# A chunked delta-rule kernel with a max-of-three feed-forward layer: a reordered opening, and 38 extra products of the identity on TensorE

## The chip, the core and the metric

The kernel runs on one core of a Trainium2 chip. A core has a matrix engine (TensorE, "PE"; its weight loads are listed as "PEld"), three engines that work element by element (VectorE "DVE", ScalarE "ACT", GpSimd "POOL"), SyncE ("SP") that only issues transfers, and DMA queues that any of them but VectorE and TensorE fill here. Each engine takes its instructions in the order of the program; between engines, semaphores keep order. The metric is the time in device microseconds (us) of one execution.

## What is computed

Inputs are q, k, v of shape (4, 8, 768, 48), that is batch, heads, steps, and width of a head, beta of shape (4, 8, 768), and four weight matrices.

```python
k_n = k / (np.linalg.norm(k, axis=-1, keepdims=True) + 1e-06)
for t in range(S):
    kt, vt, bt = (k_n[:, :, t], v[:, :, t], beta[:, :, t, None])
    y[:, :, t] = np.einsum('bhd,bhde->bhe', q[:, :, t], state)
    v_old = np.einsum('bhde,bhd->bhe', state, kt)
    state = state + bt[:, :, :, None] * np.einsum('bhd,bhe->bhde', kt, vt - v_old)
...
x = y.transpose(0, 2, 1, 3).reshape(B * S, H * D)          # 3072 tokens of 384
h = np.maximum(np.maximum(x @ w1, x @ w2), x @ w3)         # width 768
out = h @ w_out
```

Everything is in 32-bit floating point, except that the weights arrive as 64-bit numbers and are converted on the chip.

## The kernel before

**Chunks.** The 768 steps are cut into 12 chunks of 64 (`C`), two of which form one of 6 groups. Within a chunk the recurrence becomes matrix products and the inverse of a unit triangular matrix, made of the products of the chunk's keys. All 32 pairs of batch and head go through together. Group m is prepared while the feed-forward layer of an earlier group runs on TensorE; for group 0 nothing runs beside it, and its preparation is the opening of the kernel, from the first load to the first feed-forward product `p_h` (L1224) at 44.9 us.

**The order** is written out by hand (`manual_schedule`, L104 on). The lines L1281 to L1375 are the opening; then the loop over `ffn(0)` yields after each product of hidden units, and the tables `LINKS` and `FIRST` say which steps of the recurrence and of the next preparation are put in at each yield. The program's order is each engine's order.

**Preparing a unit.** `load_k`, `load_q` bring keys and queries of unit n (a chunk and half of the batches); `turn` (L322) transposes them on TensorE (against the identity `ident`) and copies the result out as `kqt`; part 0 is the keys, part 1 the queries. `gram` (L404) multiplies keys with keys into `at` (part 0) or keys with queries into `pt` (part 1). With `later=True` ACT copies `pt` out and the `mask` is applied later by `masked` (L398); otherwise VectorE masks straight from PSUM.

**The triangular solve.** `solve(m)` (L507) works on blocks of 32x32. For the group 0, `to_blocks` and `first_blocks` put the products into `x_bl`, 128 partitions x 32 x 32. Its diagonal holds the squared norms of the keys. `norm` (L268) makes the norm: a root on ACT, then on VectorE a Newton step and the added 1e-6 of the reference. Its inverse square times beta scales `x_bl` (L547) and starts the diagonal of `y_bl`. Group 0 then takes 15 steps (`HB` = 16, so two halves of 16) of two VectorE instructions each (L561, L565). After them y_bl is transposed (L573) and `placed` (L498) copies it into `ut[0]` and `ut[1]`, the two chunks' triangular matrices. The halves are joined to 32 by `halves_t` (VectorE transposes), `halves_z` and `halves_u` (TensorE products `p_e`, `p_f`, with copies), then to 64 by `turn_t1`, `join_z` and `join_u` (`p_z`, `p_j`). Later groups take 31 steps and go through DRAM: `blocks(m)` loads their blocks, for group 1 into a spare part of the weights' tile (`in_wo`).

**A chunk's step.** `scale` multiplies v by the norms on POOL (`nrm_0` for the first two chunks, made by `first_norms`); `new` makes u (`p_u`), `to_y` the outputs (`p_y`), `to_x` transposes them (`p_x`) into `xt`, the feed-forward input; `step` adds to the state `st` (`p_s`, L801), `old_k` subtracts the state's share from v (`p_k`, L755), `old_q` keeps that of the queries (`p_q`).

**Weights.** Each of 24 pieces is fetched as raw bits (`fetch`), taken apart by three ACT instructions (L247 to L249), and put together by a VectorE shift (L259) and a POOL add (L263), `joined`. The generator `weights()` is `conv`: `some(conv, 1)` does the ACT part of a piece and then joins the piece before it. `p_h` of a yield needs its piece joined.

**Fillers that exist already.** `busy(n, of)` (L1290) runs n products of the identity into a PSUM tile `p_w` that nobody reads; it is called once, with 6, before the first transposition. `p_w` shares its two PSUM buffers with `p_h`.

Of the kernel before, what the change touches and what calls it, by code (L numbers as in the profile page):

```python
# [18 lines left out]
BL = 32  # L19
# [4 lines left out]
def kernel(  # L24
# [205 lines left out]
    def weights():  # L230

        waiting = None
        for dst, _, (a, b) in pieces:
            bits = staged.popleft().rearrange("p (a b two) -> p a b two", a=a, two=2)
            low, high = bits[:, :, :, 0], bits[:, :, :, 1]
            mant = work.tile([128, 384], U32, name="mant", bufs=2)
            up = work.tile([128, 384], I32, name="up", bufs=2)
            mant_v = mant.rearrange("p (a b) -> p a b", a=a)  # L240
            up_v = up.rearrange("p (a b) -> p a b", a=a)
            halves = [
                up.bitcast(t)[:, i::2].rearrange("p (a b) -> p a b", a=a)
                for i, t in enumerate((I16, FP16))
            ]

            nc.scalar.mul(mant_v.bitcast(FP32), high.bitcast(FP32), 2.0**-112)  # L247
            nc.scalar.mul(halves[0], low, 2.0**-29)
            nc.scalar.mul(halves[1], high.bitcast(FP32), 2.0**-64)  # L249
            if waiting:  # L250
                joined(*waiting)
            waiting = dst, mant, mant_v, up_v
            yield
        joined(*waiting)
        yield
# [12 lines left out]
    def norm(out, ksum, root, t):  # L268
# [8 lines left out]
        )  # L277

# [219 lines left out]
    def placed(cc, i, copy=nc.vector.tensor_copy, xs_of=slice(0, 2 * H)):  # L498
# [6 lines left out]
        copy(to[:, xs_of], of[:, xs_of])  # L505

    def solve(m):  # L507
# [14 lines left out]
        norm(bl, diagonal(x), small("root_bl", BL), small("nt_bl", BL))  # L522
        if m == 1:
            y = ps_two("y_p").rearrange("p b (j i) -> p (b j) i", i=BL)
            nc.scalar.copy(y, zero.to_broadcast(y.shape))
        if m:
            norms_of(m, bl)
            nc.vector.reciprocal(bl, bl)
        else:
            bl_0.append(bl)  # L530
            bl = small("inv_bl", BL)
            nc.vector.reciprocal(bl, bl_0[0])
        nc.vector.tensor_tensor(out=bl, in0=bl, in1=bl, op=ALU.mult)
        nc.vector.tensor_tensor(out=bl, in0=bl, in1=beta_bl[:, m] if m else beta_0, op=ALU.mult)
# [36 lines left out]
        if m == 0:  # L571
            back = in_rows(xs[0])
            nc.vector.transpose(out=back, in_=y.rearrange("p c i -> p i c"))  # L573
            yield
            for i in range(4):
                if i % 2:
                    n = H * (i == 3)
                    if n:
                        placed(0, i, nc.vector.tensor_copy, slice(0, n))
                    placed(0, i, nc.scalar.copy, slice(n, 2 * H))  # L580
                else:
                    placed(0, i, nc.vector.tensor_copy)
            return
# [55 lines left out]
    def halves_t(c, parts=(0, 1)):  # L639
        if c not in fine:  # L640
            fine[c] = [square("t") for g in range(2)]
        src = [ut[c % NU][:, g].rearrange("p h x -> p (h x)") for g in range(2)]
        dst = [t.rearrange("p h x -> p (h x)") for t in fine[c]]
        if 0 in parts:
            nc.vector.transpose(out=dst[0], in_=src[0])
        for bb in range(2) if 1 in parts else ():
            nc.vector.transpose(out=dst[1][rows(1 - bb)], in_=src[1][rows(bb)])
# [27 lines left out]

    def halves_z(c):
        if c > 1:
            halves_t(c)
        at = [ats[2 * c + g] for g in range(2)]
        second = ut[c % NU].rearrange("p g h (f two x) -> p g h f two x", two=2, x=HB)  # L680
        for hs, p_v, copy in heads_of(c, "p_e", BL):
# [6 lines left out]
            copy(zs[c % NU][:, :, span(hs)], p_v)  # L688
# [601 lines left out]
    def busy(n, of):  # L1290
        p_w = ps_ffn([128, TOK], "p_w")[:, 0 : of.shape[1]]
        for _ in range(n):
            nc.tensor.matmul(p_w, ident, of)

# [35 lines left out]
    turn(6, (0,))  # L1330
    turn(0, (1,))
    load_q(3, (nc.gpsimd, nc.gpsimd))
    load_beta()
    keys(6)
    gram(0, (1,), None, later=True)
    turn(7, (0,))
    turn(1, (1,))
# [3 lines left out]
    turn(3, (1,))  # L1341
    some(conv, 1)
    gram(2, (1,), None, later=True)
    gram(3, (1,), None, later=True)
    some(solving, HB + 1)
    halves_t(0)
    halves_z(0)
    first_norms()
    some(conv, 1)
    placed(1, 0)  # L1350
    scale(0, nrm_0[:, 0])
    placed(1, 1, nc.gpsimd.tensor_copy)
    blocks(1, nc.gpsimd)
    for _ in range(2):
        fetch(nc.gpsimd)
    halves_u(0)
    turn_t1(0)
    join_z(0)
    masked(pts[0], by_par(pts[0]))
    placed(1, 2)  # L1360
    join_u(0)
    masked(pts[1], by_par(pts[1]))
    old_k(0)
    old_q(0)
    new(0)
    some(conv, 1)
    fetch(nc.gpsimd)
    load_v(1, nc.gpsimd)
    placed(1, 3)
    to_y(0)  # L1370
    halves_t(1)
    solving = solve(1)
    some(solving, 1)
    to_x(0)
    some(conv, 1)  # L1375
# [76 lines left out]
    for i, _ in enumerate(ffn(0)):  # L1452
# [11 lines left out]
        if i == 25:  # L1464
            some(conv, 1)
# [7 lines left out]
        if i in CONVERTED:  # L1473
            some(conv, 1)
        if i == 0:
            fetch(nc.gpsimd)
# [78 lines left out]
```

## Time and profile before

| | |
|---|---|
| median of three runs | 506.24 us (505.86 to 509.44) |
| the profiled execution | 506.9 us, span 505.2 us |
| mean granted TensorE clock | 0.968 |
| busy: PE, PEld, DVE, ACT, POOL | 484.0, 338.0, 361.1, 169.4, 187.1 us |
| first `p_h` product | 44.92 us |
| granted clock 0.50 | 18.96 to 22.38 and 25.79 to 53.1 us |

All times of the trace count from the first instruction of the span. A view by windows gives the busy time of each engine in a stretch and the clock that TensorE was granted. A timeline gives start, length, engine, line, operation, output<-input by the program's names, shape and, in brackets, the idle time of the engine before it and what ended it. A view of waits names the waiting and the releasing instruction, total time, how often, and the longest.

### The profile page before, as it was taken

The page shows a single profiled execution, that of the slowest core. Times are in us where ns is not written, and L with a number is a line of the kernel's source. Part 1 is how long each engine was busy: PE and PEld are TensorE (multiplying, and loading weights), DVE is VectorE, ACT ScalarE, POOL GpSimd, SP SyncE. Part 2 cuts the span into 40 slices and gives each one's busy share as a digit, 9 for nine tenths or more (in the row PEclk, how much of TensorE's full clock was granted, in tenths as well). Part 3 has the DMA queues.
Part 4 walks back from the last instruction along what each step waited for, and adds up shares of the span by engine and source line. Part 5 has one row for each costly group of instructions (what it writes and reads, how often), then busy time and mean ns, then how long its engine had stood idle before and what let it go on. Part 6 is the DMA issues. An engine that isn't in the chain of part 4 may idle for free.

```text
span 505.2 us, 18676 instructions
## 1 busy us (share of the span) xinstructions
PE 484.0 (96%) x8064; PEld 338.0 (67%) x8064; DVE 361.1 (71%) x835; ACT 169.4 (34%) x320; POOL 187.1 (37%) x311
## 2 busy tenths in 40 slices
PE   7678989999999999999999999999999999999996
PEld 6467767855566555565565565555797457998895
DVE  5888799787996441799652999565998874468753
ACT  5585664885422142210152200242201032212210
POOL 7434472793391935770395880501000020000000
PEclk9855899999999999999999999999999999999999
DMA  8937869864045934544584652744224230340002
GB/s 114 205 50 214 195 142 160 198 181 137 3 120 134 191 72 77 146 119 117 112 156 104 158 137 74 149 72 96 64 54 90 47 86 15 85 94 1 0 18 47
DMA packets 109121, 53.50 MB, mean 106 GB/s; under 512 B 92208, under 2 KB 102864, under 8 KB 109040
## 3 DMA queue, kind: packets, MB, share of 16 engines
q1 hardware_dynamic: 97280, 31.78, 31.0%
q0 software_dynamic: 9216, 19.85, 16.5%
q8 instruction: 63, 1.03, 0.9%
q10 hardware_dynamic: 2544, 0.69, 0.8%
q14 instruction: 18, 0.15, 0.1%
HBM read 39.17 MB, written 13.11 MB: 103 GB/s over the span
## 4 chain that ended last, share of the span: by engine, by line
PE 76%; DVE 11%; ACT 4%; DMA 3%; SPq 3%; issue 2%; POOL 0%; DVEq 0%; ACTq 0%; POOLq 0%
PE p_h L1224 28%; PE p_o L985 13%; PE p_o L1262 12%; PE p_c L1163 5%; DVE tmp L561 3%; PE p_g L415 2%; PE p_m L905 2%; PE p_u L771 2%; PE p_k L743 2%; DVE y_p L565 2%; DMA kmore<-in_k_dram 2%; PE p_y L813 2%; PE p_s L794 2%; PE p_q L743 1%; PE p_j L726 1%
## 5 line engine op out<-in xcount | busy, mean ns | idle before, releaser
L1224 PE MATMUL p_h<-xt,w_sb 128*128 128x512 f32 (+1 forms) x450 | 186.8, 558 | 0.6 <-ACT xt L839 0.6
L1224 PEld LDWEIGHTS p_h<-xt,w_sb 128*128 128x128 f32 x450 | 82.4, 193 | 69.2 <-issue 61.6
L1238 DVE TENSOR_TENSOR h<-h,p_h 128x512 f32<-128x512 f32 (+1 forms) x42 | 25.5, 607 | 46.8 <-PE p_h L1224 46.3
L565 DVE TENSOR_TENSOR y_bl<-y_bl,tmp 128x31 f32<-128x31 f32 (+20 forms) x139 | 50.4, 363 | 4.8
L561 DVE TENSOR_TENSOR tmp<-x_bl,y_bl 128x31 f32<-128x31 f32 (+20 forms) x139 | 48.8, 351 | 3.9
L1262 PE MATMUL p_o<-wo_sb,h 128*128 128x384 f32 x144 | 48.9, 490 | 0.0
L373 POOL DMA_DIRECT2D turned<-in_q_dram x72 | 39.3, 554 | 4.6 <-POOL turned L368 3.1
L1262 PEld LDWEIGHTS p_o<-wo_sb,h 128*128 128x128 f32 x144 | 26.7, 190 | 17.2
L1234 ACT ACTIVATE h<-p_h 128x512 f32<-128x512 f32 x24 | 14.3, 597 | 69.2 <-PE p_h L1224 69.2
L263 POOL TENSOR_TENSOR w_sb<-mant,up 128x384 int32<-128x384 int32 x18 | 19.0, 1054 | 39.5 <-DVE mant L259 37.8
L415 PEld LDWEIGHTS p_g<-kqt 48*64 48x64 f32 x1216 | 24.5, 142 | 9.2 <-issue 6.3
L415 PE MATMUL p_g<-kqt 48*64 48x64 f32 (+1 forms) x1216 | 27.7, 241 | 0.9 <-ACT kqt L344 0.8
L1268 ACT COPY o_sb<-p_o 128x384 f32<-128x384 f32 x12 | 5.8, 479 | 62.6 <-PE p_o L1262 56.5
L801 DVE TENSOR_TENSOR st<-st,p_s 48x768 f32<-48x768 f32 (+1 forms) x18 | 17.1, 949 | 12.7 <-PE p_s L794 12.4
L399 DVE TENSOR_TENSOR pt<-p_g,mask 128x512 f32<-128x512 f32 x20 | 13.8, 690 | 17.0 <-PE p_g L415 16.9
L598 POOL DMA_DIRECT2D ut<-y_d x4 | 2.6, 653 | 60.6 <-DMA y_d<-y_bl 60.6
L148 POOL DMA_DIRECT2D v_t<-in_v_dram x14 | 11.6, 832 | 35.3 <-PE p_u L771 35.3
L368 POOL MEMSET turned<- 128x96 f32 x18 | 3.3, 191 | 49.4 <-DVE kqt L389 49.4
L771 PEld LDWEIGHTS p_u<-v_t,ut 64*64 64x64 f32 x768 | 13.5, 141 | 8.4 <-issue 7.3
L432 ACT COPY at<-p_g 128x512 f32<-128x512 f32 x22 | 12.8, 585 | 17.4 <-DVE pt L399 15.4
L373 POOL DMA_DIRECT2D turned<-in_k_dram x32 | 17.5, 556 | 1.2 <-POOL turned L368 1.2
L1163 PE MATMUL p_c<-xt,w_sb 128*128 128x256 f32 x72 | 17.7, 379 | 0.0
(239 smaller groups left out, 907.3 us busy)
## 6 DMA issues: line engine op xcount, KB each, us to landing
w_bits<-in_moe_w_dram SPq DMA_DIRECT2D x9, 384.0 KB, 6.2
w_bits<-in_moe_w_dram POOLq DMA_DIRECT2D x9, 384.0 KB, 5.7
turned<-in_q_dram POOLq DMA_DIRECT2D x72, 48.0 KB, 2.8
out_dram<-o_sb SPq DMA_DIRECT2D x36, 96.0 KB, 2.3
y_x<-y SPq DMA_DIRECT2D x32, 96.0 KB, 3.0
qall<-y_x SPq DMA_DIRECT2D x32, 96.0 KB, 2.8
v_t<-in_v_dram POOLq DMA_DIRECT2D x14, 192.0 KB, 5.0
at_d<-at SPq DMA_DIRECT2D x72, 32.0 KB, 3.0
```

The lines of the kernel that those rows point to most:

```text
L263: nc.gpsimd.tensor_tensor(out=dst.bitcast(I32), in0=mant_v.bitcast(I32), in1=up_v, op=ALU.add)
L373: (queue, nc.gpsimd)[i].dma_start(out=t[p0 : p0 + 32, bb, at : at + NP * 2 * D].rearrange("p (j x) -> p j x", j=NP), in_=(k, q)[i][2 * bb ...
L415: nc.tensor.matmul(p_g[rows(bb ^ (g * i)), par, c0 : c0 + C * (1 + whole)], kq[:, 0], kq if whole else kq[:, i],)
L561: nc.vector.tensor_tensor(out=t_v, in0=row.to_broadcast(t_v.shape), in1=column.to_broadcast(t_v.shape), op=ALU.mult,)
L565: nc.vector.tensor_tensor(out=rest, in0=rest, in1=t_v, op=ALU.subtract)
L771: nc.tensor.matmul(p_v[rows(bb ^ g), g, i], ut[c % NU][rows(bb), g, h], rhs[rows(bb), g, h],)
L801: nc.vector.tensor_tensor(out=s_v[r], in0=s_v[r], in1=p_s[r, :, 0 : H * D], op=ALU.add)
L985: nc.tensor.matmul(to[:, g], a[j][:, 128 * g : 128 * (g + 1)], b[j], start=(start and g == j == 0), stop=(stop and g == 1 and j == len(a) ...
L1163: nc.tensor.matmul(to, w[stays], moves, start=(n == 0), stop=(n == len(terms) - 1))
L1224: nc.tensor.matmul(p_h, w_sb[i][:, t, f * 128 : (f + 1) * 128], xt[:, t, lo : lo + w], start=(t == 0), stop=(t == KT - 1),)
L1238: nc.vector.tensor_tensor(out=h, in0=h, in1=p_h, op=ALU.max)
L1262: nc.tensor.matmul(p_o, stays, moves, start=(n == 0), stop=(n == len(terms) - 1))
```

## The change

Five parts, all in group 0's opening.

- **Norms.** solve(0) no longer makes the norm first. The inverse of the squared norm-plus-epsilon comes from one root on ACT, one add and one reciprocal on VectorE (`inverse_squares`); the norms themselves, for `first_norms`, are made by `first_roots` with a root on ACT and four small instructions on POOL.
- **From the solve to `ut`.** The whole transpose of y_bl is split into two halves of the columns (`turn_back`). The high columns, which are all that `halves_z` reads, are placed first; the low ones after the products `p_e`. The transposed halves for `halves_u` come from one VectorE transpose (`turn_half`) into a spare part of `wo_sb` and eight small copies over VectorE and ACT, into tiles that POOL zeroed before (`zero_halves`). `halves_z` copies with ACT alone.
- **Order.** All four copies of `ut[1]` are made together by VectorE after `to_y(0)` (one was on POOL). `turn(3, (1,))` goes to the end of the opening, `gram(3, (1,))` into the loop (`P3` for `M3`, so that it's masked from PSUM).
- **Conversions.** `some(conv, 1)` now does ACT's part only; `join_first()` joins the oldest waiting piece and is called where the program says. Two of the opening's conversions come before the solve's end.
- **Fillers.** `busy` is defined earlier, its second argument may be left out, and it's called ten more times in the opening: 6, 5, 10, 3, 3, 4, 2, 1, 3, 1 products, 38 in all.

```diff
@@ weights, joined @@
-            if waiting:
-                joined(*waiting)
-            waiting = dst, mant, mant_v, up_v
+            waiting.append((dst, mant, mant_v, up_v))
             yield
-        joined(*waiting)
-        yield
+
+    waiting = deque()
+
+    def join_first():
+        joined(*waiting.popleft())
...
+    def inverse_squares(out, square_of, ksum):
+
+        nc.scalar.activation(
+            out=square_of, in_=ksum, func=mybir.ActivationFunctionType.Sqrt,
+            scale=4.0 * EPS * EPS,
+        )
+        nc.vector.scalar_tensor_tensor(
+            out=square_of, in0=square_of, scalar=EPS * EPS, in1=ksum,
+            op0=ALU.add, op1=ALU.add,
+        )
+        nc.vector.reciprocal(out, square_of)
+
+    def first_roots():
+
+        out, square_of, inverse = bl_0
+        t, mult = small("root_bl", BL), nc.gpsimd.tensor_tensor
+        nc.scalar.sqrt(out, square_of)
+        mult(out=t, in0=out, in1=out, op=ALU.mult)
+        mult(out=t, in0=t, in1=inverse, op=ALU.mult)
+        nc.gpsimd.tensor_scalar(
+            out=t, in0=t, scalar1=-0.5, scalar2=1.5, op0=ALU.mult, op1=ALU.add
+        )
+        mult(out=out, in0=out, in1=t, op=ALU.mult)
...
+    def turn_back(s):
+
+        cols = slice(HB * s, HB * (s + 1))
+        nc.vector.transpose(
+            out=in_rows(xs[0])[:, cols], in_=ys[0].rearrange("p c i -> p i c")[:, cols]
+        )
...
@@ placed @@
-        copy(to[:, xs_of], of[:, xs_of])
+        copy(to[:, :, cols], of[:, :, cols])
@@ solve @@
-        norm(bl, diagonal(x), small("root_bl", BL), small("nt_bl", BL))
...
         else:
-            bl_0.append(bl)
-            bl = small("inv_bl", BL)
-            nc.vector.reciprocal(bl, bl_0[0])
-        nc.vector.tensor_tensor(out=bl, in0=bl, in1=bl, op=ALU.mult)
...
+            bl_0.extend((bl, small("square_bl", BL), small("inv_bl", BL)))
+            bl = small("nt_bl", BL)
+            inverse_squares(bl_0[2], bl_0[1], diagonal(x))
...
         if m == 0:
-            back = in_rows(xs[0])
-            nc.vector.transpose(out=back, in_=y.rearrange("p c i -> p i c"))
-            yield
...
+            ys.append(y)
             return
@@ halves @@
+    def zero_halves(c):
+        fine[c] = [square("t") for g in range(2)]
+        zeros(*fine[c])
+
+    def first_half():
+        return in_wo(1)[:, 0, 0 : HB * BL].rearrange("p (c x) -> p c x", x=BL)
+
+    def turn_half():
+
+        nc.vector.transpose(
+            out=first_half().rearrange("p c x -> p (c x)"),
+            in_=ys[0][:, 0:HB].rearrange("p c i -> p (c i)"),
+        )
+
+    def halves_t(c, engines):
+        for n, engine in enumerate(engines):
+            f, bb, g = n // 4, n // 2 % 2, n % 2
+            x0 = 16 * c + 8 * g
+            copy = nc.scalar.copy if engine is nc.scalar else engine.tensor_copy
+            copy(
+                fine[c][g][block(bb ^ g, f), :, BL * f : BL * f + HB],
+                first_half()[block(bb, f), :, x0 : x0 + H].rearrange("p c h -> p h c"),
+            )
+    def busy(n, of=None):
+
+        of = ident if of is None else of
+        p_w = ps_ffn([128, TOK], "p_w")[:, 0 : of.shape[1]]
+        for _ in range(n):
+            nc.tensor.matmul(p_w, ident, of)
@@ opening @@
     turn(6, (0,))
+    busy(6)
     turn(0, (1,))
     load_q(3, (nc.gpsimd, nc.gpsimd))
     load_beta()
+    first_roots()
+    zero_halves(0)
+    zero_halves(1)
     keys(6)
     gram(0, (1,), None, later=True)
     turn(7, (0,))
+    some(conv, 1)
+    busy(5)
     turn(1, (1,))
     keys(7)
     turn(2, (1,))
     gram(1, (1,), None, later=True)
-    turn(3, (1,))
     some(conv, 1)
     gram(2, (1,), None, later=True)
-    gram(3, (1,), None, later=True)
-    some(solving, HB + 1)
-    halves_t(0)
+    busy(10)
+    some(solving, HB)
+    low, high = slice(0, HB), slice(HB, BL)
+    turn_back(1)
+    for i in range(4):
+        placed(0, i, A.copy if i % 2 else V.tensor_copy, high)
+    turn_half()
+    halves_t(0, (V, A, V, A, V, A, V, V))
     halves_z(0)
+    turn_back(0)
+    for i in (1, 3, 0, 2):
+        placed(0, i, V.tensor_copy, low)
+    busy(3)
+    halves_u(0)
+    turn_t1(0)
     first_norms()
-    some(conv, 1)
-    placed(1, 0)
+    join_first()
     scale(0, nrm_0[:, 0])
-    placed(1, 1, nc.gpsimd.tensor_copy)
     blocks(1, nc.gpsimd)
     for _ in range(2):
         fetch(nc.gpsimd)
-    halves_u(0)
-    turn_t1(0)
+    busy(3)
     join_z(0)
     masked(pts[0], by_par(pts[0]))
-    placed(1, 2)
+    busy(4)
     join_u(0)
     masked(pts[1], by_par(pts[1]))
+    busy(2)
     old_k(0)
     old_q(0)
     new(0)
     some(conv, 1)
+    join_first()
     fetch(nc.gpsimd)
     load_v(1, nc.gpsimd)
-    placed(1, 3)
+    busy(1)
     to_y(0)
-    halves_t(1)
+    for i in (0, 2, 3, 1):
+        placed(1, i)
+    halves_t(1, (V, V, V, V, V, V, V, V))
+    busy(3)
     solving = solve(1)
+    to_x(0)
+    join_first()
+    busy(1)
+    some(conv, 1)
     some(solving, 1)
-    to_x(0)
-    some(conv, 1)
+    turn(3, (1,))
@@ loop over ffn(0) @@
-        3: "j1 S1 q1 M3 S1 S1", 4: "u1 T4", 5: "y1", 6: "s1 T5", 7: "x1 T6",
+        3: "j1 S1 q1 P3 S1 S1", 4: "u1 T4", 5: "y1", 6: "s1 T5", 7: "x1 T6",
...
         if i == 25:
-            some(conv, 1)
+            join_first()
...
         if i in CONVERTED:
             some(conv, 1)
+            join_first()
```

More of the change, by code (lines that the diff above doesn't have):

```diff
@@ L230, in weights @@
     def weights():
-        waiting = None
         for dst, _, (a, b) in pieces:
@@ L277, in norm @@
         )
+    EPS = 1e-6
+    def inverse_squares(out, square_of, ksum):
[18 more added lines that the diff above has]
+        mult(out=out, in0=out, in1=t, op=ALU.mult)
     def small(name, *shape):
@@ L495, in blocks, with placed @@
         )
-    def placed(cc, i, copy=nc.vector.tensor_copy, xs_of=slice(0, 2 * H)):
+    ys = []
+    def turn_back(s):
[3 more added lines that the diff above has]
+        )
+    def placed(cc, i, copy=nc.vector.tensor_copy, cols=slice(0, BL)):
         bb, half = divmod(i, 2)
@@ L521, in solve @@
         bl = small("bl", BL)
-        norm(bl, diagonal(x), small("root_bl", BL), small("nt_bl", BL))
-        if m == 1:
-            y = ps_two("y_p").rearrange("p b (j i) -> p (b j) i", i=BL)
-            nc.scalar.copy(y, zero.to_broadcast(y.shape))
         if m:
+            norm(bl, diagonal(x), small("root_bl", BL), small("nt_bl", BL))
+            if m == 1:
+                y = ps_two("y_p").rearrange("p b (j i) -> p (b j) i", i=BL)
+                nc.scalar.copy(y, zero.to_broadcast(y.shape))
             norms_of(m, bl)
             nc.vector.reciprocal(bl, bl)
+            nc.vector.tensor_tensor(out=bl, in0=bl, in1=bl, op=ALU.mult)
         else:
-            bl_0.append(bl)
-            bl = small("inv_bl", BL)
-            nc.vector.reciprocal(bl, bl_0[0])
-        nc.vector.tensor_tensor(out=bl, in0=bl, in1=bl, op=ALU.mult)
-        nc.vector.tensor_tensor(out=bl, in0=bl, in1=beta_bl[:, m] if m else beta_0, op=ALU.mult)
+            bl_0.extend((bl, small("square_bl", BL), small("inv_bl", BL)))
+            bl = small("nt_bl", BL)
+            inverse_squares(bl_0[2], bl_0[1], diagonal(x))
+        nc.vector.tensor_tensor(
+            out=bl, in0=bl if m else bl_0[2], in1=beta_bl[:, m] if m else beta_0,
+            op=ALU.mult,
+        )
         if m > 2:
@@ L571, in solve @@
         if m == 0:
-            back = in_rows(xs[0])
-            nc.vector.transpose(out=back, in_=y.rearrange("p c i -> p i c"))
-            yield
[L575 to L582, printed above, removed]
+            ys.append(y)
             return
@@ L637 @@
     fine = {}
[L639 to L647, printed above, removed]
+    def zero_halves(c):
[16 more added lines that the diff above has]
+                first_half()[block(bb, f), :, x0 : x0 + H].rearrange("p c h -> p h c"),
+            )
     def heads_of(c, name, w):
@@ L674, in span @@
         return slice(hs[0], hs[-1] + 1)
+    def busy(n, of=None):
[3 more added lines that the diff above has]
+            nc.tensor.matmul(p_w, ident, of)
     def halves_z(c):
-        if c > 1:
-            halves_t(c)
         at = [ats[2 * c + g] for g in range(2)]
@@ L687, in halves_z @@
                     )
-            copy(zs[c % NU][:, :, span(hs)], p_v)
+            nc.scalar.copy(zs[c % NU][:, :, span(hs)], p_v)
     def halves_u(c):
@@ L1288 @@
     nc.scalar.sqrt(warm, warm)
[L1290 to L1293, printed above, removed]
     def keys(n, queues=one_queue, copy=nc.scalar.copy):
```

## The prediction

> **What bounds the kernel now.** I read the slices of the span first, then the stages, then the waits and the rows of the opening.
>
> ```profile
> PE   7678989999999999999999999999999999999996
> DVE  5888799787996441799652999565998874468753
> PEclk9855899999999999999999999999999999999999
> ```
>
> TensorE is full from the eighth slice on, but in slices 2 to 4 (12.6 us each) it has gaps and a low granted clock. Whatever the change does before 90 us, the rest follows as a block of constant length. Windows of the busy time in four stages (sum and mean left out) say who sets the pace before that; columns are start:end, length, busy us of PE, PEld, DVE, ACT, POOL, clock, DMA:
>
> ```profile
> 26.43:44.93 18.50, 13.93 (x447) 12.42 (x442) 16.27 (x28) 14.71 (x35) 9.42 (x10) 0.50 0.40 105
> 44.93:56.86 11.93, 11.93 (x273) 10.04 (x274) 7.60 (x24) 5.78 (x13) 5.03 (x6) 0.66 0.88 207
> 56.86:88.50 31.64, 28.26 (x640) 23.24 (x643) 29.62 (x79) 19.42 (x36) 13.93 (x17) 1.00 0.88 159
> 88.50:135.00 46.50, 46.35 (x1040) 29.86 (x1032) 39.20 (x76) 31.82 (x62) 28.77 (x36) 1.00 0.53 140
> ```
>
> First stage: a relay from the first triangular solve to the first feed-forward product, with VectorE 88% busy. Second: TensorE busy throughout at two thirds of its clock, VectorE waiting. Third: VectorE 94% busy, the rest being the 0.03 us between instructions (79 rows). Fourth: TensorE. So the time is set by when VectorE gets to 56.86, where v_t's subtraction (L755) ends and the second solve starts in earnest. VectorE's waits in 44 to 60:
>
> ```profile
> DVE st L801 <- PE p_s L794: 1.9, 1, 1.9
> DVE v_t L755 <- PE p_k L743: 1.6, 1, 1.6
> DVE h L1238 <- PE p_h L1224: 0.3, 1, 0.3
> ```
>
> These 3.8 us are what TensorE's half clock costs the queue that counts. The same windows at the clock's own steps:
>
> ```profile
> 15.55:18.96 3.41, 2.14 (x72) 1.59 (x70) 2.78 (x11) 2.63 (x5) 1.93 (x3) 1.00 1.25 217
> 18.96:22.38 3.42, 3.42 (x56) 2.64 (x60) 3.03 (x11) 1.53 (x3) 2.27 (x5) 0.50 1.35 224
> 22.38:25.79 3.41, 0.87 (x32) 0.70 (x24) 3.02 (x12) 0.81 (x2) 0.00 (x0) 1.00 1.10 199
> ...
> 46.27:49.68 3.41, 3.41 (x76) 2.58 (x78) 3.10 (x10) 0.41 (x2) 0.00 (x0) 0.50 0.89 197
> 49.68:53.09 3.41, 3.41 (x72) 3.05 (x65) 1.48 (x5) 2.14 (x4) 3.19 (x3) 0.50 0.84 149
> 53.09:56.51 3.42, 3.42 (x135) 2.93 (x135) 1.50 (x4) 1.54 (x5) 1.74 (x2) 1.00 0.85 234
> ```
>
> The clock changes only at multiples of 3.41 us, each step answering to the window before it. Busy time doesn't sort these windows: 46.27 is 100% busy and the clock stays low. What does: each matmul instruction's streamed columns times the share of the 128x128 array it uses (rows x columns / 16384). A 128x128 one counts 128, p_h's 256 columns 256, p_g 12, p_e and p_f 8, p_u and p_y 12, p_z and p_j 2. Windows that left the clock low sum to 1408 at most (15.55, and 42.86); those that left it high to 1472 (18.96), 1696 (49.68), later 1792 and more. My bar is therefore 1408 to 1472 a window.
>
> **The change part by part.** *The norm chain of solve(0).*
>
> ```profile
> 14.62 0.18 DVE L271 TENSOR_SCALAR nt_bl<-root_bl 128x32 f32<-128x32 f32 x1 [0.32 <-ACT root_bl L270]
> ...
> 16.70 0.19 DVE L534 TENSOR_TENSOR inv_bl<-inv_bl,beta 128x32 f32<-128x32 f32 x1 [0.21 <-DMA kmore<-in_k_dram]
> 16.93 0.69 DVE L547 TENSOR_TENSOR x_bl<-x_bl,inv_bl 128x512 f32<-128x512 f32 x1
> ```
>
> Seven VectorE instructions stand between ACT's root and L534; two remain (an add like L274, 0.19, and a reciprocal, 0.35). Starts were 0.22 and 0.39 apart for these, so beta's product starts near 15.25 instead of 16.70. The "DMA" there isn't one that must be awaited: beta's last transfers were issued at 8.7 and took 3.8 to 5.0, so landed by 13.7; the 0.21 is four semaphore instructions 0.1 apart, which stay. Gain 1.45: the solve ends at 24.98, not 26.43. POOL's copy to the diagonal (0.69) still lies beside L547 (0.69). The square roots moved to POOL (four instructions of 0.7, by L538) and the four zeroed tiles (0.48 each, by 0.98 for twice the width) fill POOL's idle 12.6 us before L263; needed at 27.6, they are done by about 25. If they weren't, up to 1 us would show.
>
> *From the solve's end to p_u.* A half transpose (1.0) and two copies of 32x256 (VectorE 0.37, ACT 0.63 each) let p_e start at 27.3 instead of 30.13; ACT's weight conversion and pt copies, which stood in front of its share, are earlier. Then VectorE's own list is in the way: the second transpose 0.71, five copies of 32x128 (0.26 by the line through 0.37 and 0.59), the other half transpose 1.0, four copies 1.6, two negations 0.62, t1's transposes 1.4. So the norms reach POOL at about 34, as before, and POOL still adds (1.2) before scaling v_t:
>
> ```profile
> 34.97 1.47 POOL L296 TENSOR_TENSOR v_t<-v_t,nrm 128x768 f32<-128x768 f32 x1
> 36.50 1.03 POOL L505 COPY ut<-x_bl 32x512 f32<-32x512 f32 x1
> ```
>
> p_u can't start before 37.1 (before: 38.1). Behind the scaling, POOL loses the 1.03 copy, so its block read and two weight fetches (37.48 and 38.08, landing 5.7 later) move by 0.2 at most: the fourth conversion on ACT, and behind it solve(1)'s root, wait for the fetch until 43.7 and end near 45.4; the zeroing of y_p, turn(3)'s copy and the first h copy queue up behind, and TensorE's third p_h for that copy's PSUM. No DMA passes another on SP, and turn(3) issues none.
>
> *VectorE to the second norm.* Against its 16.27: second transpose +0.71, placed(0) 2.2 for 1.6, halves_t(0) 1.3 for 2.15, z's copy (to ACT) -0.42, placed(1) whole +0.59, halves_t(1) eight copies 2.1 for 2.15, a join's shift +0.35: 17.2. With 40 gaps of 0.03 (1.2) and waits of 2.0 for p_u, which wait on POOL, it takes 20.4, not 18.5; the norm starts at 45.4, not 44.93: all of the 1.45 is spent. Bounds: the small copy costs 0.15 (the line's foot) to 0.37 (the row itself), 13 of them, so -1.4 to +1.4; the wait for p_u vanishes at best (-2.0). I take the line, being between two rows.
>
> *Clock and fillers.* A product of the identity is two matmul rows. At the start six took 2.93, 0.49 each, at half clock (p_t's four took 0.89 there, 0.63 later). At full clock half of p_h's 256-column row (1.56 for six) gives 0.26; bounds 0.22 (eight p_t in 1.09, less the tail) and 0.30. All 38 are 9.9 us; 21 go before the solve's end, where TensorE's queue loses turn(3)'s 2.5 us wait for q, and end near 25.6; of the 17 behind it (4.4), those ahead of p_z, p_j and p_y lie in waits for negations, z and u. At half clock they would be 8.3 us and not fit. Each counts 256: 9728 in all, on top of 7300 real in the eight windows from 15.55, 2100 a window against a bar of 1440. On average the clock holds; the thin spot is 25 to 29 us (p_e 512, three fillers 768: 1280).
>
> With the clock full, TensorE has p_s ready before VectorE asks and p_k 1.1 us after st: the 3.8 us of waits go. Norm to L755's end was 11.93, becomes 8.0: 53.4, not 56.86. **Sum: 56.86 - 53.4 = 3.4 us.** gram(3) and turn(3), now inside the third stage, cost TensorE 1.4 us of its 3.4 idle there and VectorE nothing (a mask from PSUM 0.69 for one of 1.03). The profiled execution took 506.9 (span 505.2, 1.7 around it): 503.5; the median of the three runs is 0.7 lower, so 502.8.
>
> Two rules bear on it. Beside the rows' steps of 3.41 us stands the Trainium skill, TensorE: Matmul & The Clock Gate, "Part 1: The HAM clock gate": the window runs free of the kernel's start, so a fixed number of warm-up products means little, and the ramp is worth under 1% of a typical span. That speaks against 38 placed by hand; by it the whole clock is worth at most 5 us. In window 18.96, 896 of the 1472 are transposes and the clock rose after it; the same page's "Part 4: PE-mode transpose" says transposes don't engage the gate. The measurement decides for counting them; by the rule only windows before 25 would be weaker, and fillers alone (1280 to 2560) nearly carry those.
>
> **The rivals.**
> *The clock drops for a while* in the thin spot or at 34 to 37. For: 1280 is under the bar, and where the steps fall in another run isn't known. Against: three quarters of a filler more would do. p_u and p_y at half clock (2.1 against 1.15 in the rows) put 1 to 2 us back: 504.3 to 506.
> *VectorE is lighter than I think*: the 2.0 wait for p_u shrinks and copies are at their low bound. 3.4 + 1.7 to 3.4: 499.5 to 501.2. Against: POOL's order is unchanged.
> *Slower: the clock falls at 29 and stays low to the loop*, as it does now, and fillers of 0.49 stand in the chain. p_z 0.4 later, p_j 2.1, p_u1 0.9 and twice as long, y 3.2: the norm at 48.6, and from there 11.93 as now, so L755 ends at 60.5, 3.7 late: 510. It decides as soon as the norm plus the returned waits pass 56.86, that is with the clock low in four windows running.
>
> **How the numbers follow.** Main case 0.48 (own range 501.2 to 504.6), a partial drop 0.22, lighter VectorE 0.18, slower 0.12. About 1% (5.1 us, 501.2 and 511.3) can be told from no change: faster 0.21 (the lighter case and a little of the main one), slower 0.09 (the upper part of the last case: fillers before 25 at half clock too would add 1 to 2 us), same 0.70. The range 499.5 to 509 leaves out about 0.13.
>
> **What would show it.** L534's successor near 15.3; the solve's end near 25.0; clock 1.00 in every window from 5.3; p_e at 27.3 but p_u not before 37; the second norm near 45.4; no wait for p_s or p_k; the third stage as long as now. A norm well before 45, or a clock of 0.50 after 30, makes the number wrong.

## The result and the profile after

| | before | after |
|---|---|---|
| median | 507.03 us (505.86 to 509.68, 6 runs) | 515.24 us (513.16 to 518.32, 6 runs) |
| ratio, 95% interval | | 1.0159 [1.0125, 1.0192] |
| profiled execution | 506.9, span 505.2 | 516.76, span 515.0 |
| mean granted clock | 0.968 | 0.981 |

The change made the kernel slower by 1.6%, though the mean of the recorded clock went up. The records begin with the clock's first rise, at 5.31 us before and at 14.65 after. Ahead of it products take as long as at half clock (the six products of the identity at 2.0 us took 2.93, the six at 17.0 took 1.50); with that time counted as half, the means are 0.963 and 0.967, nearly the same. From the page of the kernel after, the slices of the span (12.9 us each) and the queue that the argument needs (packets, MB, share):

```profile
PE   8889689999999999999999999999999999999996
...
DVE  3887879787988351399762799554998873477752
...
PEclk9979789999999999999999999999999999999999
...
q8 instruction: 64, 1.05, 0.9%
```

The clock of slices 3 and 4 is up, as wanted (5 and 5 before), that of slices 5 and 6 down. In slice 5 TensorE is now 60% busy, where it was 90% or more. The same four stages as before, from the solve's end to the first p_h, to the end of v_t's subtraction (L802 now), to the second solve's end, and 46.5 us more:

```profile
27.96:46.50 18.54, 16.08 (x434) 14.27 (x433) 13.74 (x30) 10.66 (x28) 8.30 (x9) 0.82 0.42 104
46.50:60.13 13.63, 9.34 (x273) 7.92 (x272) 12.18 (x34) 7.46 (x17) 4.89 (x5) 0.83 1.05 184
60.13:94.39 34.26, 30.92 (x655) 25.42 (x657) 29.16 (x79) 18.37 (x34) 13.88 (x17) 0.92 0.78 145
94.39:140.89 46.50, 44.30 (x1050) 29.20 (x1043) 37.71 (x75) 31.51 (x62) 28.58 (x35) 1.00 0.55 143
```

Lengths were 18.50, 11.93 and 31.64, and the rest of the span 416.7; now it is 420.6. The first stage begins 1.53 late. In the second the roles are swapped: VectorE, whose list of the opening now reaches to 50.0, 3.5 us behind the first p_h, is 12.18 us busy of 13.63 (7.60 of 11.93 before) and TensorE waits. VectorE's waits from 44 to 62, then TensorE's longest from 20 to 75 (two views: waiting, releaser, total, times, longest):

```profile
DVE y L864 <- PE p_y L860: 1.6, 1, 1.6
DVE v_t L802 <- issue: 0.7, 1, 0.7
```

```profile
PE p_k L790 <- DVE st L848: 3.9, 1, 3.9
```

Of VectorE's 3.8 us of waits for p_s, p_k and h, 0.7 are left: the wait put down to "issue" ends at 59.18, where p_k ends (59.05). In place of the others TensorE waits 3.9 us for VectorE. What that does to the clock, in windows at its steps:

```profile
55.62:59.03 3.41, 1.94 (x65) 1.85 (x65) 2.75 (x8) 0.00 (x0) 0.74 (x1) 0.50 1.14 199
59.03:62.44 3.41, 3.41 (x54) 2.40 (x54) 3.09 (x10) 1.56 (x3) 1.15 (x3) 0.50 0.49 134
...
65.86:69.27 3.41, 1.22 (x45) 0.92 (x38) 0.90 (x4) 3.37 (x7) 0.99 (x1) 1.00 0.51 134
69.27:72.68 3.41, 3.41 (x38) 2.39 (x41) 3.04 (x8) 0.16 (x1) 0.83 (x1) 0.50 0.02 5
```

Behind each thin window here the next one is at half clock, and it is full of dense p_h products, which then take longer (2.93 us for six, 1.56 at full clock). The window at 65.86 is thin for a reason that the forecast had not looked for. TensorE's timeline there:

```profile
64.89 1.15 PE L790 MATMUL p_q<-st,kqt 48*64 48x48 f32 x64
67.22 0.34 PE L441 MATMUL p_g<-kqt 48*64 48x64 f32 x8 [1.19 <-ACT ut L775]
68.57 0.58 PE L441 MATMUL p_g<-kqt 48*64 48x64 f32 x24 [1.00 <-issue]
69.08 2.78 PE L1271 MATMUL p_h<-xt,w_sb 128*128 128x256 f32 x6
```

These p_g are the Gram products that the change moved into the loop, and VectorE masks them straight from PSUM. Its longest wait in the third stage, before and then after:

```profile
DVE tmp L561 <- ACT wo_sb L567: 0.3, 1, 0.3
```

```profile
DVE pt L425 <- PE p_g L441: 2.5, 1, 2.5
```

That is nearly the 2.6 us by which the stage grew.

**The stops.** In the middle of the 32 equal products TensorE stops for 1.00 us and waits for nothing that the profile knows ("issue"). A row below is one instruction in TensorE's program. All 63 such stops of 0.6 us or more in the 20 profiles of this study lie at the same kind of place: with all of TensorE's rows counted in order of start (weight loads, products and some 130 others), each is ahead of row 193 plus a multiple of 256, give or take two. The queue named "instruction" moved 64 packets of 16,384 bytes after and 63 before, and TensorE's 16,414 and 16,261 rows divided by 256 are 64.1 and 63.5: TensorE's program arrives in blocks of 256 rows, 64 bytes a row. (The Trainium skill, "Perfetto Trace Analysis", "The 4-stage abstract model", gives an instruction 64 bytes, which agrees.) The times of some fetches, put together from that queue's packets and TensorE's rows:

```
kernel  rows of the block  entered  next block's fetch  used up  goes on  stop
before  2497 to 2752        60.94     62.88 to 64.38      64.64    65.65   1.01
after   2497 to 2752        64.28     65.90 to 67.07      67.57    68.57   1.00
after   5313 to 5568       133.09    134.00 to 134.94    135.22   136.32   1.11
```

At the stops, the fetch of the next block began up to 6.3 us after the block was entered (the three above: 0.9 to 1.9), took 0.9 to 1.8, and the engine went on 1.2 to 1.8 us after its end. What delays a fetch's start isn't seen. A block that lasts longer than these together hides the fetch; the three above, small products for the most part, lasted 2.1 to 3.7 us. One filler is four rows (two weight loads, two products), so 38 are 152 rows, which move every later boundary to other instructions. Stops of this kind cost 1.0 us before and 5.2 us after up to 145 us.

**A sum over the whole span.** TensorE is 96% busy, so its account is the kernel's: span = idle time + what half clock cost (half of the busy time at 0.50, the time ahead of the first rise included) + the busy time that the work would take at full clock. From the page's span and busy time, and the granted clock:

| us | span | idle | half clock | work at full clock |
|---|---|---|---|---|
| before | 505.2 | 21.2 | 14.7 | 469.3 |
| after | 515.0 | 21.8 | 13.8 | 479.4 |
| e1 (after, no fillers) | 512.1 | 26.3 | 17.2 | 468.6 |
| e5 (before, 38 near-empty products) | 514.1 | 19.9 | 22.8 | 471.4 |
| e13 (after, rows made up to a block) | 511.1 | 20.8 | 8.5 | 481.8 |
| e17 (after's chain, mended, no fillers) | 505.9 | 20.9 | 15.1 | 469.9 |
| e18 (e17 with fillers) | 506.3 | 18.0 | 6.9 | 481.4 |

The fillers are 10 to 12 us of TensorE work. From before to after the span grows by 9.8 us: 10.1 of work, 0.6 of idle time, 0.9 less of half clock. In the first 45 us idle time and half clock together did shrink, from 23.4 us to 15.8; behind them they grew from 12.5 to 19.9.

### The profile page after: what moved, and what is told of

Read it like the earlier page. It is cut to its first block, busy times and chain, and to the rows that moved or that the text cites. A ratio compares the mean times of both kernels' runs of the same rounds, so it can differ in the third digit from the quotient of the medians.

```text
span 515.0 us, 18845 instructions
## 1 busy us (share of the span) xinstructions
PE 493.2 (96%) x8140; PEld 346.9 (67%) x8140; DVE 361.0 (70%) x842; ACT 169.3 (33%) x324; POOL 188.3 (37%) x318
## 4 chain that ended last, share of the span: by engine, by line
PE 88%; DMA 3%; DVE 3%; issue 2%; SPq 2%; ACT 1%; POOL 1%; ACTq 0%; POOLq 0%; DVEq 0%
PE p_h L1271 34%; PE p_o L1032 12%; PE p_o L1309 12%; PE p_c L1210 5%; PE p_g L441 4%; PE p_u L818 3%; PE p_k L790 2%; PE p_m L952 2%; PE p_y L860 2%; PE p_q L790 2%; PE p_s L841 2%; PE p_z L760 2%; DMA v_t<-in_v_dram 2%; PE p_j L773 1%; SPq L129 1%
## 5 line engine op out<-in xcount | busy, mean ns | idle before, releaser
L1309 PEld LDWEIGHTS p_o<-wo_sb,h 128*128 128x128 f32 x144 | 26.7, 190 | 17.2
L790 PEld LDWEIGHTS p_k<-st,kqt 48*64 48x64 f32 x672 | 11.9, 143 | 9.9 <-DVE st L848 4.1
L246 ACT ACTIVATE mant<-w_bits 128x384 f32<-128x384 f32 x24 | 13.5, 563 | 14.1 <-POOL w_sb L263 7.0
L399 POOL DMA_DIRECT2D turned<-in_k_dram x32 | 17.5, 553 | 1.4 <-POOL turned L394 1.2
```

The source lines that it names most:

```text
L399: (queue, nc.gpsimd)[i].dma_start(out=t[p0 : p0 + 32, bb, at : at + NP * 2 * D].rearrange("p (j x) -> p j x", j=NP), in_=(k, q)[i][2 * bb ...
L790: nc.tensor.matmul(p_b[rows(bb), par, c0 : c0 + D], kqt[g][dims(par), j, bb ^ g, i], st[dims(par), bb ^ g, g, j],)
L1309: nc.tensor.matmul(p_o, stays, moves, start=(n == 0), stop=(n == len(terms) - 1))
```

## The experiments

Ratios are to before, in runs on the same chip. F is the theory of the instruction blocks, A that of the engines' queues, B that of the fillers' own cost.

**Undoing one part each, and the fillers alone.** e1 takes the ten calls out; e2 puts the last query block's Gram products back into the opening; e3 puts the copies of `ut[1]` back to their old places; e4 adds the ten calls to before.

```diff
@@ e1, all ten @@
-    busy(6)
@@ e2 @@
+    gram(3, (1,), None, later=True)
-        3: "j1 S1 q1 P3 S1 S1"
+        3: "j1 S1 q1 M3 S1 S1"
@@ e3 @@
+    placed(1, 0)
     scale(0, nrm_0[:, 0])
+    placed(1, 1, nc.gpsimd.tensor_copy)
...
-    for i in (0, 2, 3, 1):
-        placed(1, i)
@@ e4, on before, the same ten @@
+    busy(6)
```

> The changed kernel without the 38 products. Theory A (the loss sits in VectorE's and ACT's queues between the solve and the fifth p_h; the fillers hold the clock part of the time and are worth a little): 516 to 519 us, clock 0.50 for most of 25 to 50 us, p_s and p_k waits back. Theory B (the fillers themselves cost the time, 9.4 us of TensorE's busy time): 506 to 510 us. Theory C (the early start of the opening's chain was lost to the clock's first window, by chance of phase): no change by removing them, 514 to 516, and the start at 12.3 or 15.2 differs from run to run.

> The changed kernel with gram(3) back in the opening (after turn(3), copied by ACT) and only its mask in the loop. Theory A: VectorE's 2.5 us wait for that product in the loop goes, and the low clock behind it: 511.5 to 513.5 us. Theory B: as the changed kernel, 514.5 to 516. Theory C: the same as B.

> The changed kernel with the four copies of ut[1] where they were before (three on VectorE between the joins, one on POOL). Theory A: VectorE reaches the second norm 2 to 2.5 us sooner: 512 to 513.5 us. Rival, that the norm waits for ACT's conversion and the weights' fetch: 515 to 516, with a gap on VectorE ahead of the norm.

> The kernel before with the same 38 products at the nearest places, nothing else changed. Theory A: the clock is held for most of 19 to 45 us, the 3.8 us that VectorE waited for p_s, p_k and p_h mostly go: 503 to 505.5 us. Theory B: the products lengthen the chain: 510 to 515 us.

Measured: e1 512.07 us, 1.0098 [1.0061, 1.0136]; e2 518.33, 1.0228 [1.0188, 1.0267]; e3 518.24, 1.0216 [1.0172, 1.0260]; e4 513.90, 1.0126 [1.0092, 1.0160]. e2, e3 and e4 missed A's ranges; e4 lies in B's, e1 between A's and B's, and C's for e1 (514 to 516) was missed. Putting a part back made it worse by 3 us twice, so A as it stood had fallen. The fillers alone cost before 6.4 us. Where, shows in e4's TensorE timeline:

```profile
61.14 0.84 PE L743 MATMUL p_q<-st,kqt 48*64 48x48 f32 x41
66.18 0.89 PE L743 MATMUL p_q<-st,kqt 48*64 48x48 f32 x23 [4.20 <-issue]
67.00 2.93 PE L1224 MATMUL p_h<-xt,w_sb 128*128 128x256 f32 x6
```

A stop of 4.20 us at a block's boundary (entered at 58.71, fetched from 63.32 to 64.82), and p_h behind it at half clock: 2.93 for 1.56. These four runs led to theory F.

**Rows with little work.** e5 is e4 with each filler cut to 32x32 against one column; e6 to e8 add 16, 32 and 48 such products to after.

```diff
@@ e5 @@
-            nc.tensor.matmul(p_w, ident, of)
...
+                nc.tensor.matmul(p_w[0:32, 0:1], ident[0:32, 0:32], ident[0:32, 0:1])
@@ e6; e7: 32, e8: 48 @@
             nc.tensor.matmul(p_w, ident, of)
+        for _ in range(16 if n == 10 else 0):
+            nc.tensor.matmul(p_w[0:32, 0:1], ident[0:32, 0:32], ident[0:32, 0:1])
```

> The kernel before with the 38 products of the run e4_before_fill at the same places, but each cut to a tile of 32x32 against one column: the same 152 TensorE rows (two weight loads and two products each), at a few hundredths of a microsecond for one (f32 products of 48x64 take 0.69 us for 32 rows, so 38 about 1.6 us, nearly all in waits), and next to no activity for the clock. Theory F (TensorE's instruction blocks: its program comes in blocks of 256 rows, each fetched when the one before is entered, and 152 rows move every later boundary to other work, where a block of short products can be used up before the next one has landed): 510 to 514, with idle stretches of 0.5 to 4 us put down to issue at rows 193 above a multiple of 256, as in e4. Theory B (the fillers cost by the time they take or by the clock they change): 506.5 to 508.5, as before, with no more such stretches than before's one of 1.01 us.

> The kernel after with 16 products of 32x32 against one column behind the group of ten, in TensorE's wait for the first solve: 64 more TensorE rows, some 0.5 us of work inside a wait, nothing else. Theory F: every block boundary behind it falls 64 rows earlier in the program, so the stalls of 1.00, 1.15, 1.09 and 1.11 us of the profile after go or move, and the time leaves 515.2 by 1.5 us or more, to either side (the three runs with 16, 32 and 48 lie over 3 us apart). Theory A (the queues of VectorE and ScalarE decide) and theory B: 514.5 to 516, all three alike within 1.5 us.

> The same with 32 products: 128 more TensorE rows. Theory F: boundaries 128 rows earlier than after's; a time over 1.5 us from that of at least one of the runs with 16 and 48. Theories A and B: 514.5 to 516.5.

> The same with 48 products: 192 more TensorE rows. Theory F: boundaries 192 rows earlier than after's; a time over 1.5 us from that of at least one of the runs with 16 and 32. Theories A and B: 514.5 to 517.

Measured: e5 516.39, 1.0140 [1.0079, 1.0200]; e6 512.32, 1.0077 [1.0042, 1.0112]; e7 515.46, 1.0119 [1.0083, 1.0154]; e8 515.55, 1.0167 [1.0082, 1.0252]. e5 lies above F's range (510 to 514) and far above B's. Near-empty products cost before as much as full ones, so the full fillers' columns and their clock aren't needed for the loss. They aren't free, though: the 38 took some 5 us of TensorE in e5's profile, where 1.6 had been expected. e5's timeline:

```profile
59.26 0.62 PE L713 MATMUL p_z<-ut,at 32*32 32x32 f32 x48
62.30 0.44 PE L713 MATMUL p_z<-ut,at 32*32 32x32 f32 x16 [2.43 <-issue]
62.67 2.93 PE L1224 MATMUL p_h<-xt,w_sb 128*128 128x256 f32 x6
```

One stop of 2.43 us, then three windows at half clock, from 61.9 to 72.2. e6 lies 2.9 us below after, e7 and e8 at after's time; e6 to e8 lie 3.2 us apart, F's bound, but their runs scatter by 6 to 12 us each, so of after's alignments this says only that they matter by a few us at most.

**A whole block of rows.** On before, n near-empty products in one place ahead of p_e: 64 are one block, so that boundaries fall as in before.

```diff
+    rows_of(64)     # e9; e10: 38, e11: 16
     some(solving, HB + 1)
```

> The kernel before with 64 products of 32x32 against one column in one place, right ahead of the opening's first p_e, in TensorE's wait for the first solve: 256 more TensorE rows, one whole block, so that every block boundary behind them falls at the same instruction as in before. They are about as much work again as the 38 of e5_before_tiny (some 2 us, in a wait). Theory F (the rows count by where they put the block boundaries): 506.5 to 509, within 1.5 us of before. Theory G (any further rows, or the small products themselves, cost): at least e5's 6 to 8 us, so 513 to 518.

> The same with 38 products in that one place: 152 more TensorE rows, boundaries moved by as many rows as in e5, though fewer products. Theory F: 511 to 517, over 3 us above the run with 64. Theory G: between before and the run with 64, in proportion to the products.

> The same with 16 products: 64 more rows. By the profile of before its blocks of under 4.2 us (a fetch, its latency and the restart) add up to 0.7 us too short when the boundaries are moved by 64 rows, 2.3 us unmoved, 3.4 us moved by 152, between rows 900 and 6000. Theory F: 504.5 to 507.5, at or below before. Theory G: 508 to 510, a quarter of what the run with 64 loses.

Measured: e9 512.58, 1.0100 [1.0033, 1.0167]; e10 517.11, 1.0211 [1.0153, 1.0270]; e11 513.96, 1.0121 [1.0047, 1.0196]. 64 cost less than 38, against G's proportion, but far more than F said, and 16 as much as 64, which neither said (its four runs lie from 511.3 to 519.6). For the 64, most is my price for them, as e9's timeline shows:

```profile
28.73 1.99 PE L415 MATMUL p_g<-kqt 48*64 48x64 f32 x64
30.65 6.98 PE L1298 MATMUL p_w<-ident 32*32 32x1 f32 x128
37.56 1.94 PE L685 MATMUL p_e<-ut,at 64*64 64x32 f32 x64
```

Two instructions each, all into one column, took 0.11 us a product at half clock, not "a few hundredths"; 7 us didn't fit into before's wait of 2.2 for p_e, which starts 8.1 us behind the solve's end for 3.7: 4.4 of the 5.1 us that e9 lost. 38 took 4.2 us in e10 (2.0 over the wait) and 16 took 1.9 in e11, which fit; e11's loss isn't explained by them. The rows' own mark is cleaner behind the opening. TensorE's waits from 76 to 140 us, in e9 and in e10:

```profile
PE p_u L771 <- DVE v_t L755: 0.9, 1, 0.9
PE p_z L713 <- DMA ut<-y_d: 0.4, 2, 0.2
```

```profile
PE p_q L743 <- issue: 2.3, 2, 1.7
PE p_s L794 <- issue: 0.8, 1, 0.8
```

No stop with 256 rows more; 3.1 us of them with 152. Stops of 0.15 us or more at boundaries behind 75 us, summed over each profile, by rows added modulo 256 (over all 20 profiles):

```
  0 rows: before 0, e1 0.4, e9 0, e12 0, e13 0, e15 0, e16 0, e17 0
152 rows: after 4.1, e2 4.5, e3 3.0, e4 2.5, e5 1.9, e10 4.6
others:   e6 (216) 1.4, e7 (24) 2.5, e8 (88) 3.2, e11 (64) 2.0, e14 (40) 2.5, e18 (40) 0.7
```

**The parts of the chain.** e12 is before with the new norm alone, the roots behind it on ScalarE and GpSimd. e13 is after with 26 near-empty products (104 rows and the fillers' 152 are 256). e14 is after with the fillers as 10 products of 512 columns, 40 rows. e15 is e1 with turn(3) and gram(3) back in the opening, e16 that with the copies of `ut[1]` in their old places.

```diff
@@ e12, on before @@
+    first_roots()
...
-        norm(bl, diagonal(x), small("root_bl", BL), small("nt_bl", BL))
...
+            inverse_squares(bl_0[2], bl_0[1], diagonal(x))
@@ e14 @@
-        of = ident if of is None else of
+            of = kpad[0].rearrange("p h d -> p (h d)")[:, 0:512]
+            n = {6: 2, 5: 1, 10: 3, 4: 1, 3: 1}.get(n, 0)
@@ e15, on e1 @@
+    turn(3, (1,))
     some(conv, 1)
     gram(2, (1,), None, later=True)
+    gram(3, (1,), None, later=True)
...
-    turn(3, (1,))
...
-        3: "j1 S1 q1 P3 S1 S1"
+        3: "j1 S1 q1 M3 S1 S1"
```

> The kernel before with the first solve's norm as in the kernel after (the square of the reciprocal taken without the roots ahead of the solve, the roots off the path on ScalarE and GpSimd), and nothing else of the change: TensorE's rows and their order are those of before. The prediction priced it at 1.45 us less on the path to the first solve's end (24.98 for 26.43 us). Theory F, by which the rest of the opening's worth is lost to where the block boundaries and with them the stalls fall: 504.5 to 507.5. The rival, that a shorter opening moves TensorE's short products to where fetches are slower, as in e1: 508 to 512.

> The kernel after with 26 products of 32x32 against one column behind the group of ten: 104 TensorE rows, which with the 152 of the 38 fillers make 256, one whole block, so that behind the opening the block boundaries fall where they would fall without any filler. Theory F: the stalls behind 75 us go (3.35 us between 75 and 150 us and 0.79 at 338 us in the profile after), 510.5 to 512.5. Theory B (the fillers' time, 38 at 0.24 us) and theory A (the order of VectorE's work): 514 to 516.5, as after.

> The kernel after with its 38 fillers made of 10 products of the identity with 512 columns of a loaded key tile: as many columns, so as much TensorE time and activity for the clock, in 40 rows for 152. By the profile after, boundaries moved back by 112 rows leave blocks under 4.2 us that are 1.1 us too short in all, for 4.8 as they are. Theory F: 509 to 512. Theory B: 514 to 516.

> The kernel after without the 38 fillers, and with the last query block's turn and Gram products put back where before has them, in the opening: TensorE's rows and their order are now those of before to the last one; the shortened chain of the opening and the order of VectorE's copies are those of after. Theory F: TensorE's stalls as in before, little of them, and what the shorter chain is worth shows: 504 to 508, against 512.07 of e1. Theory A (VectorE's longer list ahead of the second norm decides): 510 to 513.

> The same, and the four copies of the second chunk's solve tile back in their old places, one of them on GpSimd: of the change the norm, the solve's split end and the earlier conversions remain. Theory F: as e15 within 2 us. Theory A: 2 to 4 us under e15, 505 to 509, as the second norm comes before v_t's subtraction by as much as in before.

Measured: e12 507.16, 1.0002 [0.9969, 1.0035]; e13 513.95, 1.0145 [1.0091, 1.0200]; e14 513.14, 1.0104 [1.0064, 1.0144]; e15 510.68, 1.0063 [1.0032, 1.0093]; e16 510.63, 1.0051 [1.0026, 1.0077].

e12 is in F's range and not in its rival's, but the interval is as wide as the 1.45 us that were to be gained. The new norm does what was forecast (the solve ends at 24.95 for 26.40); no gain shows, since TensorE's p_e waits for ScalarE's share of the copies and starts at 31.11, for 30.13 before. ScalarE's timelines, before and e17, whose solve ends at 24.83:

```profile
27.96 1.05 ACT L426 COPY pt<-p_g 128x512 f32<-128x512 f32 x2
29.03 1.70 ACT L505 COPY ut<-x_bl 32x512 f32<-32x512 f32 x2
```

```profile
28.09 1.04 ACT L452 COPY pt<-p_g 128x512 f32<-128x512 f32 x2
29.16 1.28 ACT L540 COPY ut<-x_bl 32x256 f32<-32x256 f32 x2
```

With no idle time between, ScalarE's list begins with the copy of the last query block, which TensorE can turn at 25.34 and 25.52 only, behind its load; ut follows at 29.0 and 29.2 (30.0 in e12), however early the solve ends.

e13 did to the stops what F said (none behind 75 us) but not to the time: 1.3 us under after, with intervals that overlap. Its 26 products also took 1.8 us in front of p_e. e14 is 2.1 us under after, between the two theories. That would fit if the moved rows were a part of the fillers' cost and their time another; it isn't shown. e15 is 1.4 us under e1, short of F and within A's range; but e16 doesn't bear A out, as the copies of `ut[1]` in their old places are worth nothing. In e16 the chain's gain stops at p_u; GpSimd's timeline, then TensorE's:

```profile
36.57 1.81 POOL L263 TENSOR_TENSOR w_sb<-mant,up 128x384 int32<-128x384 int32 x1 [12.64 <-DMA at_d<-at]
38.35 1.82 POOL L322 TENSOR_TENSOR v_t<-v_t,nrm 128x768 f32<-128x768 f32 x1
```

```profile
40.22 1.96 PE L818 MATMUL p_u<-v_t,ut 64*64 64x48 f32 x64 [3.01 <-POOL v_t L322]
```

The join's add stands ahead of the scaling on GpSimd and waits for VectorE's shift at 36.11; the norms' turn, ahead of that on VectorE, comes at 35.97 (33.19 before).

**Mending that, and fillers on top.**

```diff
@@ e17, on e16 @@
     halves_z(0)
+    first_norms()
+    scale(0, nrm_0[:, 0])
...
-    first_norms()
     join_first()
     placed(1, 0)
-    scale(0, nrm_0[:, 0])
@@ e18, on e17: seven places, 10 products of 512 columns in all @@
+    busy(2)
```

> The kernel of e16, with the turn of the first norms on VectorE and the scaling of v_t on GpSimd put back right behind the opening's first p_e, ahead of the low half's copies and ahead of the join of the first converted weights. Theory H (the shortened chain ends at p_u, where TensorE waits 3.01 us for the scaling): that wait goes to under 0.5 us, p_u starts 2 to 3 us sooner after the solve's end than in e16 (there 14.9 us after it), and the time falls by 1.5 to 3 us, to 507.5 to 509. Rival (the wait is slack: VectorE's norm and state behind p_x set the rest): p_u earlier, the time as e16 within 1 us, 509.6 to 511.6.

> The same with 10 products of the identity with 512 columns in the waits, the activity of the 38 fillers in 40 TensorE rows (e14's, in seven of its places). Theory B (the fillers' own time, some 9 us of TensorE at full clock, is worth no more than the idle and half-clock time that it takes away): 1 us under e17 to 3 us over it. The change's own idea (activity in the waits keeps the clock up, to TensorE's gain): 2 to 4 us under e17.

Measured: e17 509.47, 1.0016 [0.9987, 1.0045]; e18 514.34, 1.0110 [1.0061, 1.0158]. In e17 the scaling ends at 30.78, p_u starts at 37.82, 13.0 us behind the solve's end for 14.9, and the time comes down by 1.2 us, a little less than forecast and within the intervals, to that of before. e18 missed both ranges: fillers cost e17 4.9 us in the median. Its profiled execution is its fastest (508.38; the others 510 to 519): there 11.5 us of fillers took 11.1 us from idle time and half clock (from the table above), which is no gain at best. Why its other runs are so much longer isn't seen, since only one execution has a trace.

**Where the fillers cost.** Three pairs of profiles, without and with fillers:

| | v_t's subtraction ends | from there to the second solve's end | rest of the span |
|---|---|---|---|
| before, e4 | 56.86, 56.84 | 31.64, 35.75 | 416.7, 419.7 |
| e1, after | 58.64, 60.13 | 36.62, 34.26 | 416.9, 420.6 |
| e17, e18 | 57.65, 57.13 | 31.62, 31.62 | 416.6, 417.5 |

All fillers have run by 47 us. Up to v_t's subtraction they cost nothing in the first and the last pair, and in the second 1.1 of the 1.5 us are another matter (L585, below). What grew lies behind them, where no filler runs any more, but every block boundary has moved. Single profiles differ by some 2 us there, though: the rest is 418.7 to 418.9 in e12, e13 and e15 too, which have no stops behind 75 us.

**The ladder.** From after down to before, each step's ratio: 1.0159; without fillers 1.0098; turn and Gram products back 1.0063; copies back 1.0051; scaling early 1.0016. The first step and the whole are clear of their intervals, and so are the last three steps taken together (1.0098 to 1.0016); each of these alone is not. Nothing tried beat before.

## Why the prediction was wrong

- **The solve's end at 25.0.** Right where only that changed (24.95 in e12). The profile after has 27.96 because the clock first rose at 14.65 there, for 5.3: x_bl's transpose at 15.18 for 12.31. That is chance, not the change: e2, e3 and e13, with the same start, rose by 6.3, and e9, with before's, at 17.3. The medians need not carry it.
- **p_e at 27.3,** 2.3 behind the solve's end. Right but for the start: 1.8 behind it in after and e1, 2.3 in e2.
- **p_u not before 37.1, held by GpSimd.** Right but for the start, in mechanism and size: GpSimd's scaling ends at 40.24 and p_u starts at 40.34, 12.4 behind the solve's end, where 12.1 were forecast. In e2 it starts at 37.08.
- **The second norm at 45.4.** It came at 50.01. 3.0 us are the late start and 0.3 p_u. The other 1.4 lie behind p_u: VectorE waited 4.1 us on the way to the norm (1.9 for p_j, 0.6 for u, 1.6 for y), where 2.0 were forecast.
- **The 3.8 us of waits go, "11.93, becomes 8.0".** 3.1 of the 3.8 went, but v_t's subtraction ended 10.1 us behind the norm. Two of VectorE's instructions took longer beside GpSimd's, L585 2.29 for 1.22 and L273 0.71 for 0.21, and 0.7 went to waiting for p_k, which ran at half clock (1.96 for 1.13). In e1, where L585 took 1.22, the subtraction ended 8.4 behind the norm.
- **The clock holds.** In part: 0.50 from 31.7 to 38.5, behind the thin spot, and again in two places behind 55 that had no fillers. Nor does the bar of 1408 to 1472 sort the windows of after: counted in the same way, the window at 7.83 has 1600 and the next was at half clock, that at 59.03 has 1368 and the next was at full clock.
- **"The third stage as long as now" and "the rest follows as a block of constant length".** This is the step that failed: 34.26 for 31.64, and 420.6 for 416.7. gram(3), moved into the third stage, was to cost "VectorE nothing"; VectorE waited 2.5 us for it. Behind the fillers TensorE was taken to be ready whenever its inputs and its clock were. Each filler was priced by its time (0.26 forecast, 0.25 measured: 2.50 us for ten in e13) and its columns, never by its four rows, and all 9.9 us of them were put at nothing. With them taken out again (e1), 0.6% of the 1.6% comes back; the rest of the span is then 416.9, as before, while the third stage, with gram(3) still in it and other stops, is 36.62.

Against its 503.5 us, the profiled execution is 13.3 us late: 4.6 at the norm (3.0 of them chance), 2.1 to v_t's subtraction, 2.6 in the third stage, 3.9 behind. The rival on the slow side had the sign, not the mechanism: the clock didn't stay down at 29.

What is shown: the fillers cost (e1 under after, e4 and e18 over what they were added to); near-empty products cost as much on before (e5), though not only by their rows; the stops behind 75 us follow the rows modulo 256 in all 20 profiles; with the fillers, the moved turn and Gram products, the copies and the scaling all undone (e17), the time is before's. What is only argued: how the 1.0% that e1 still loses divides among the last three, how after's fillers divide into rows and time, since e13 and e14 lie within a few us of both, and how much of the 45 to 75 us stops is chance, as these differ from run to run with the same rows (1.0 us in before, 4.7 in e12).

## What to carry to other kernels

Where one engine is busy for 96% of the span, work that is put into its waits must be set against what it takes from idle time and from half clock over the whole span, not at the spot; here 10 to 12 us bought 11 at best. Count what an edit does to the number of instructions on the engine, not only to its time: here every stop of 0.6 us or more marked "issue" on TensorE was the program's next block arriving late, and rows added early moved these stops everywhere behind. When a chain is shortened, look up what stands first in the in-order list of every engine that must touch its result.

## What was not expected of the hardware

- TensorE's program comes during the run in blocks of 256 rows, and where the block before is used up first, TensorE stands still; these stops reached 4.20 us. One page of the Trainium skill, "Trainium Architecture — The Big Picture", "The software stack", says that the instruction streams are brought into each engine's memory when the program is loaded. Here the instruction queue's 64 packets, spread over the span, show that TensorE's program is fetched as it runs; the measurement decides.
- In one set of executions the clock first rose at any time from 5.3 to 17.5 us, which moves the opening by up to 3 us.
- VectorE's product of 128x1024 (L585) took 2.29 us in the profile after, where GpSimd's scaling had started 0.26 us ahead of it, and 1.22 in every other profile. In e17 it started 0.13 us ahead of the scaling, and the scaling took 2.42 us for 1.47: the later of the two was held up.
- A near-empty product (two instructions into one column) took 0.11 us at half clock; 32 instructions of 48x64 with 64 columns take 0.69 us at full clock, 0.02 each.
